# A weight load cut in two, and 26 idle matmuls moved from the tail into a wait

## The chip, the cores and the metric

The kernel runs on one core of a Trainium2 chip. The metric is the device time of one execution in microseconds. A core has TensorE (matmuls, PE in the profile), VectorE (DVE), ScalarE (ACT), GpSimd (POOL) and SyncE (SP), and 16 DMA engines that move data between the device's memory and the core.

## The reference

Two independent attention blocks, A and B, each decode one token, and their outputs are joined. Each has 32 heads of width 128 and 8192 cached keys and values per head:

```python
q = (x @ wq).reshape(B, Sq, H, Dh).transpose(0, 2, 1, 3)       # x: 1x1x512, wq: 512x4096
scores = einsum("bhqd,bhkd->bhqk", q, k_cache) * Dh ** -0.5     # k_cache: 1x32x8192x128
p = softmax(scores)
o = einsum("bhqk,bhkd->bhqd", p, v_cache)
out = o.transpose(0, 2, 1, 3).reshape(B, Sq, H * Dh) @ wo       # wo: 4096x512
```

All inputs are bf16. The caches of both blocks are 268 MB, the four weights 17 MB.

## The kernel before, in words

The 64 heads are handled in 16 rounds (`N`) of four heads (`G`), first A's eight groups and then B's. A group of K or V is 8 MB, held as 128 partitions with 64 KB each: 32 partitions (`HP`) per head, 256 keys (`T`) per partition.

Everything that is loaded in bulk goes through SP's DMA queue in the order in which SP issues it. The exception is wq of B, which ScalarE issues (its queue is q10 in the profile, SP's is q1). SP's order is: wq of A (`load_wq`, into the first half of `vn`), the two x rows, K of groups 0 and 1, and then by turns a V (`load_v`) and a K (`load_k`), each behind a wait for the buffer that it writes. K has two buffers (`kn`), V has one (`vn`). V of round n+1 is issued when the product with V of round n is done (`c_pv`), K of round n+2 when the scores of round n are done (`c_red`). At the end come wo of A, which goes into the first K buffer, the last V, and wo of B in six pieces (16, 8, 4, 2, 1 and 1 heads).

At the start TensorE turns x around (L399), waits for wq of A and multiplies (L413); ScalarE copies the queries, broadcast over partitions, into `qflat` (L368). `qflat` shares its memory with `yc`, which is used once at the end.

A round then goes like this:

- VectorE multiplies K in place with the query (L279), in two halves.
- TensorE sums that product over most of the head width with matmuls against the identity (L430, into `rps`), and VectorE sums the rest (L307).
- Maximum over the keys, across VectorE and TensorE (L312, L470, L314, L472); ScalarE takes the exponential into `pt` (L379) and its row sums.
- TensorE sums the row sums (L478), waits for V (`s_v`), and multiplies with V in 64 matmuls into `acc` (L483).
- VectorE scales and selects the result of the round before (L284 to L296), with a matmul on TensorE in between (`total_of_group`, L436).

In the last round TensorE also lays out A's and most of B's outputs and multiplies A's with wo (`mid`, L443). Behind the loop stands the tail: the first 16 heads of B with wo (L443), the function `turn_over`, `total_of_group` for the last group, and the other heads of B with wo (L505), which wait for each piece of wo in turn. VectorE and ScalarE copy the result out (L349, L384), and SP stores it (L232).

`turn_over(n)` runs n matmuls of 128x512 into `rps`, which nobody reads. Semaphores set all waits: a DMA adds 16 to its semaphore when all of it has landed.

Of the kernel before, what the change touches and what calls it, by code (L numbers as in the profile page):

```python
# [11 lines left out]
P = 128  # L12
# [33 lines left out]
def bass_concat_heads__mha_block_cached__gqa_block_cached__decode_kernel(  # L46
# [16 lines left out]
    wqs = [A_wq, B_wq]  # L63
# [4 lines left out]
    NOUT = wos[0].shape[1]  # L68
# [9 lines left out]
    N = NA * GA  # L78
# [5 lines left out]
    HM = T // 2  # L84
    W = 4
    NG = T // W


    WOB = [(0, 16, True), (16, 8, True), (24, 4, True), (28, 2, False), (30, 1, False), (31, 1, False)]
# [3 lines left out]
    with ExitStack() as st:  # L93
# [3 lines left out]
        def sb(name, shape, dt):  # L97
            return ec(nc.sbuf_tensor(name, shape, dt))

        KS = T * Dh  # L100
        kn = sb("kn", [P, 2 * KS], BF16)
        vn = sb("vn", [P, KS], BF16)
        kslot = [kn[:, i * KS:(i + 1) * KS].rearrange("p (t d) -> p t d", d=Dh) for i in range(2)]
        WQ = C * H * Dh
# [3 lines left out]
        qflat = qmem[:].bitcast(BF16)  # L108
# [10 lines left out]
        ident = sb("ident", [P, P], BF16)  # L119
# [16 lines left out]
        def ps(name, shape):  # L136
            return ec(nc.psum_tensor(name, shape, F32))

        rps = ps("rps", [P, 2, 512])
# [8 lines left out]
        def sem(name):  # L148
            return ec(nc.semaphore(name))

        s_x, s_woa, s_v, s_out = (sem(n) for n in ("s_x", "s_woa", "s_v", "s_out"))
        s_w = [sem("s_w%d" % a) for a in range(NA)]
# [25 lines left out]
            e.memset(pt[:], 0.0).then_inc(c_pool, 1)  # L178
        NPOOL = 8

        def load_wq(e, a):
            e.dma_start(vn[:, a * WQ:(a + 1) * WQ],
                        wqs[a].rearrange("(p c) n -> p (c n)", p=P)).then_inc(s_w[a], 16)


        @block.sync
        def _(e):
            load_wq(e, 0)
            for a in range(NA):
                e.dma_start(xrow[a:a + 1, :], xs[a][0]).then_inc(s_x, 16)  # L190

            def group(x, n):
                a, i = divmod(n, GA)
                return x[a][0, G * i:G * (i + 1)].rearrange("h (p t) d -> (h p) (t d)", p=HP)

            def load_k(n):
                if n >= 2:
                    e.wait_ge(c_red, RED * (n - 1))
                e.dma_start(kn[:, n % 2 * KS:(n % 2 + 1) * KS], group(ks, n)).then_inc(s_k[n % 2], 16)

            def load_v(n):
                if n:
                    e.wait_ge(c_pv, n + 1)
                else:
                    e.wait_ge(c_q, N)
                e.dma_start(vn[:], group(vs, n)).then_inc(s_v, 16)

            def load_wob(g):
                h0, n, rows = WOB[g]
                src = wos[1][h0 * Dh:(h0 + n) * Dh, :]  # L210
                dst = kn[:, WO + h0 * NOUT:WO + (h0 + n) * NOUT]
                if rows:
                    src = src.rearrange("(p j) n -> p (j n)", p=P)
                elif n > 1:
                    src = src.rearrange("(j p) n -> p j n", p=P)
                    dst = dst.rearrange("p (j n) -> p j n", j=n)
                e.dma_start(dst, src).then_inc(s_wob[g], 16)

            load_k(0)
            load_k(1)  # L220
            for n in range(N - 1):
                load_v(n)
                if n + 2 < N:
                    load_k(n + 2)
            e.wait_ge(c_red, RED * (N - 1))
            e.dma_start(kn[:, 0:WO], wos[0].rearrange("(p j) n -> p (j n)", p=P)).then_inc(s_woa, 16)
            load_v(N - 1)
            for g in range(len(WOB)):
                load_wob(g)
            e.wait_ge(c_yd, 1)  # L230
            e.wait_ge(c_ya, 2)
            e.dma_start(out[0].rearrange("o (a n) -> (o a) n", a=NA), out_sb[:]).then_inc(s_out, 16)  # L232
            e.wait_ge(s_out, 16)

        def once(e):

            one = e.alloc_register("once")
            e.reg_mov(one, 1)
            return nc.Fori(0, e.snap(one), engines=[e.engine], hint_back_edge=True)
# [111 lines left out]

        @block.scalar
        def _(e):
            load_wq(e, 1)
            with once(e):
                w_q = _Stepped(e, c_q, 1, 1)
                w_bc = _Stepped(e, c_bc, 1, 1)
                w_nb = _Stepped(e, c_nb, 1, 1)
                w_pv = _Stepped(e, c_pv, 1, 1)
                e.wait_ge(c_pv, 1)  # L360
                e.copy(xT[:].rearrange("p (a c) -> p c a", c=C),
                       misc[:, 0:C * NA].rearrange("p (c a) -> p c a", a=NA)).then_inc(c_qa, 2)
                with e.Fori(0, N // 2) as r:
                    for j in range(2):
                        w_q()
                        for h in range(G):
                            p = slice(h * HP, (h + 1) * HP)
                            i = e.copy(qflat[p, bass.ds(r * (2 * Dh) + j * Dh, Dh)],  # L368
                                       yps[j][p, h * Dh:(h + 1) * Dh])
                        i.then_inc(c_qa, 1)  # L370
                e.wait_ge(c_pool, NPOOL)
                with e.Fori(0, N):
                    w_bc()
                    e.activation(negb[:], bmp[:, 0:G], AF.Copy, scale=-scale).then_inc(c_nb, 1)  # L374
                    w_nb()
                    w_pv()
                    for h in range(G):
                        p = slice(h * HP, (h + 1) * HP)
                        e.activation(pt[p, 0:T, h], s_sb[p, :], AF.Exp, bias=negb[p, h:h + 1], scale=scale,  # L379
                                     accum_out=rsum[p, h:h + 1]).then_inc(c_p, 4)  # L380
                e.wait_ge(c_y, 1)
                e.copy(yc, yps[0][:]).then_inc(c_ya, 1)
                e.wait_ge(c_y, 2)
                e.copy(out_sb[:, NH:NOUT], yps[1][HP:HP + NA, 0:NH]).then_inc(c_ya, 1)  # L384
# [3 lines left out]
        def _(e):  # L388
            with once(e):
# [8 lines left out]
                for c in range(C):  # L398
                    i = e.matmul(misc[:, c * NA:(c + 1) * NA], xrow[:, c:D:C], ident[0:NA, 0:NA],  # L399
                                 start=True, stop=True)  # L400
                i.then_inc(c_pv, 1)
                e.wait_ge(s_w[0], 16)
                with e.Fori(0, N // 2) as r:
                    with e.If(r == GA // 2):
                        e.wait_ge(s_w[1], 16)
                    a = r // (GA // 2)
                    w0 = r * (2 * G * Dh) + a * (WQ - H * Dh)
                    x0 = a * C
                    for j in range(2):
                        e.wait_ge(c_qa, by_tile)  # L410
                        e.reg_add(by_tile, by_tile, 1)
                        for c in range(C):
# [3 lines left out]
                                start=(c == 0), stop=(c == C - 1))  # L416
# [17 lines left out]
                def total_of_group():  # L434
                    e.wait_ge(c_st, by_round)
                    e.matmul(mtp[:, EX:EX + G], om[1][:], selh[:], start=True, stop=True).then_inc(c_ex, 1)  # L436
# [21 lines left out]
                def turn_over(n):  # L458

                    with e.Fori(0, n):  # L460
                        e.matmul(rps[:, 0, :], ident[:], kn[:, 0:512], start=True, stop=True)  # L461

                with e.Fori(0, N) as r:
                    with e.Fori(0, NB // 2):
                        for tile in range(2):
                            scores(tile)
                            e.reg_add(koff, koff, HT * Dh - Dh)
                    e.reg_alu(koff, koff, 2 * KS - 1, op=ALU.bitwise_and)
                    e.wait_ge(c_g, by_round)
                    e.matmul(mtp[0:1, 0:P], m1[:], ident_f[:], start=True, stop=True).then_inc(c_gx, 1)  # L470
                    e.wait_ge(c_gm, by_round)
                    e.matmul(bmp[:, 0:G], ones_f[0:1, :], gm[:], start=True, stop=True).then_inc(c_bc, 1)  # L472
                    with e.If(r > 0):
                        total_of_group()
                    with e.If(r == N - 1):
                        mid()
                    e.wait_ge(c_p, by_round)
                    e.matmul(misc[:, 0:G], ones_f[:], rsum[:], start=True, stop=True)  # L478
                    e.wait_ge(s_v, by_round)
                    e.reg_add(by_round, by_round, 16)  # L480
                    for g in range(NG):
                        k = g % G * HP
                        m = e.matmul(acc[k:k + HP, :], ptf[:, g * W * G:g * W * G + HP],  # L483
                                     vn[:, g * W * Dh:(g + 1) * W * Dh], start=(g < G), stop=(g >= NG - G))
                    m.then_inc(c_pv, 1)
# [3 lines left out]
                for h in range(H, H + WOB[0][1]):  # L489
                    m = partial(h)  # L490
                m.then_inc(c_y, 1)
                turn_over(5)
                total_of_group()
                e.wait_ge(c_ya, 1)
                for b in range(2):
# [2 lines left out]
                for g in range(1, len(WOB)):  # L498
                    h0, n, rows = WOB[g]
                    e.wait_ge(s_wob[g], 16)  # L500
                    for h in range(h0, h0 + n):
                        for b in range(2):
                            if h == H - G - 1 and b:
# [3 lines left out]
                                         stop=(h == H - 1), skip_group_check=True)  # L507
# [29 lines left out]
```

## Time and profile before

| | |
|---|---|
| three runs | 664.8, 665.21, 665.95 us; median 665.21 |
| span of the profiled execution | 663.5 us |
| what lies around the span (median less span) | 1.7 us |
| read from the device's memory | 285.21 MB, 430 GB/s over the span |
| TensorE busy | 385.8 us (58%) |
| VectorE busy | 362.5 us (55%) |
| ScalarE busy | 76.6 us (12%) |
| critical chain, by engine | DMA 72%, PE 22%, DVE 2% |

The time of the profiled execution as such is not shown; its span, from the first to the last instruction, is. A row of a stage table gives the stage, its length, each engine's busy time with the number of instructions, the granted clock of TensorE (1.00 is full), the mean busy share of the 16 DMA engines, and what they moved. Over stages of a few microseconds that share and that rate swing, since a packet is put down to one moment; over ten and more they are steady. A row of the timeline gives start, duration, engine, line and operands, and in brackets the idle time before it and what ended that.

### The profile page before, as it was taken

What the parts mean: (1) busy time and instruction counts of PE and PEld (TensorE: products, weight loads), DVE (VectorE), ACT (ScalarE), POOL (GpSimd) and SP (SyncE); (2) the same over time, 40 slices, a digit from 0 to 9 for tenths busy, and PEclk for the clock granted to TensorE, in tenths of its full rate; (3) what the DMA queues carried; (4) which work ended last, traced back from release to release, by engine and by line L of the source; (5) the groups of instructions that cost most, each with busy time, mean ns of one, the idle gap of its engine ahead of it and who ended that gap; (6) DMA issues with size and microseconds to landing.
All of it is one profiled execution on the core that took longest, in us unless ns stands there. A gap on an engine that the chain in (4) does not pass through costs nothing.

```text
span 663.5 us, 7942 instructions
## 1 busy us (share of the span) xinstructions
PE 385.8 (58%) x2402; PEld 191.8 (29%) x2402; DVE 362.5 (55%) x249; ACT 76.6 (12%) x212; POOL 2.3 (0%) x12
## 2 busy tenths in 40 slices
PE   0455685854819185481918548191854819185488
PEld 0122232423315042330404233140423314032233
DVE  1009494848292754829274482927548292744821
ACT  0370202020010202001020200102020010202002
POOL 1000000000000000000000000000000000000000
PEclk9995988786959678695967869596786959678697
DMA  9999998999999999999999999999999999999997
GB/s 379 443 442 442 442 442 379 442 442 442 442 442 442 391 431 442 442 442 442 442 399 423 442 442 442 442 442 411 411 442 442 442 442 442 415 407 442 440 444 317
DMA packets 6041, 285.23 MB, mean 430 GB/s; under 512 B 660, under 2 KB 1176, under 8 KB 1304
## 3 DMA queue, kind: packets, MB, share of 16 engines
q1 hardware_dynamic: 5896, 281.03, 98.0%
q10 hardware_dynamic: 144, 4.19, 1.5%
q14 instruction: 1, 0.01, 0.0%
HBM read 285.21 MB, written 0.00 MB: 430 GB/s over the span
## 4 chain that ended last, share of the span: by engine, by line
DMA 72%; PE 22%; DVE 2%; issue 2%; ACT 1%; ACTq 0%; DVEq 0%; SPq 0%
DMA vn<-in_B_v_cache_dram 34%; DMA vn<-in_A_v_cache_dram 34%; PE acc L483 14%; PE rps L430 5%; DMA xrow<-in_B_x_dram 3%; PE yps L413 2%; DVE kn L279 1%; ACT qmem L368 1%; PE yps L443 1%; ACT pt L379 0%; PE yps L505 0%; DVE s_sb L307 0%; PE rps L461 0%; PE misc L478 0%; PE rps L424 0%
## 5 line engine op out<-in xcount | busy, mean ns | idle before, releaser
L279 DVE TENSOR_TENSOR kn<-kn,qmem 128x16384 bf16<-128x16384 bf16 x32 | 276.7, 8688 | 55.2 <-ACT qmem L368 43.0
L430 PE MATMUL rps<-kn,ident 128*128 x1024 | 236.8, 383 | 0.4
L483 PE MATMUL acc<-vn,pt 128*32 128x512 bf16 x1024 | 92.3, 531 | 145.7 <-DMA vn<-in_B_v_cache_dram 75.3
L307 DVE TENSOR_REDUCE s_sb<-rps 128x64 f32<-128x512 f32 x64 | 44.1, 691 | 165.1 <-PE rps L430 165.1
L430 PEld LDWEIGHTS rps<-kn,ident 128*128 128x128 bf16 x1024 | 96.4, 98 | 111.0 <-issue 22.6
L483 PEld LDWEIGHTS acc<-vn,pt 128*32 128x32 bf16 x1024 | 60.3, 127 | 171.1 <-issue 155.9
L374 ACT ACTIVATE negb<-bmp 128x4 f32<-128x4 f32 x16 | 2.8, 173 | 539.7 <-PE bmp L472 539.7
L379 ACT ACTIVATE pt<-s_sb,negb 32x256 bf16<-32x256 f32 x64 | 54.9, 858 | 4.3 <-ACT negb L374 2.9
L478 PE MATMUL misc<-rsum,ones_f 128*128 128x4 f32 x32 | 9.4, 365 | 56.4 <-ACT pt L379 56.4
L284 DVE TENSOR_SCALAR om<-acc,msk 128x128 f32<-128x128 f32 x16 | 5.6, 350 | 42.8 <-PE acc L483 42.8
L478 PEld LDWEIGHTS misc<-rsum,ones_f 128*128 128x128 f32 x32 | 8.0, 312 | 58.6 <-ACT pt L379 57.8
L413 PE MATMUL yps<-vn,xT 128*128 x64 | 17.3, 419 | 6.2 <-ACT qmem L368 4.2
L287 DVE SCALAR_TENSOR_TENSOR om<-acc,msk,om 128x128 f32<-128x128 f32 x48 | 16.8, 351 | 5.9
L470 PE MATMUL mtp<-ident_f,m 128*1 128x128 f32 x32 | 6.1, 270 | 22.6 <-DVE m L312 22.6
L424 PE MATMUL rps<-ones_bf,zrow 1*128 1x1 bf16 x64 | 11.0, 171 | 13.4 <-DVE kn L279 10.8
L424 PEld LDWEIGHTS rps<-ones_bf,zrow 1*128 1x128 bf16 x64 | 5.8, 91 | 40.6 <-issue 40.6
L368 ACT CAST qmem<-yps 32x128 f32 x64 | 16.4, 256 | 7.0 <-PE yps L413 6.3
L379 ACT ACTIVATION_READ_ACCUMULATOR pt<-s_sb,negb 32x1 f32 x64 | 15.9, 249 | 0.0
L399 PE MATMUL misc<-ident,xrow 2*128 2x2 bf16 x4 | 0.3, 166 | 22.8 <-DMA xrow<-in_B_x_dram 22.8
L413 PEld LDWEIGHTS yps<-vn,xT 128*128 x64 | 6.6, 103 | 16.5 <-issue 13.7
L472 PE MATMUL bmp<-gm,ones_f 1*128 1x4 f32 x32 | 6.1, 258 | 7.3 <-DVE gm L314 7.3
L470 PEld LDWEIGHTS mtp<-ident_f,m 128*1 128x1 f32 x32 | 1.4, 80 | 30.5 <-DVE m L312 30.5
(58 smaller groups left out, 57.0 us busy)
## 6 DMA issues: line engine op xcount, KB each, us to landing
vn<-in_B_wq_dram ACTq DMA_DIRECT2D x1, 4096.0 KB, 21.9
vn<-in_A_wq_dram SPq DMA_DIRECT2D x1, 4096.0 KB, 21.7
kn<-in_A_wo_dram SPq DMA_DIRECT2D x1, 4096.0 KB, 27.4
kn<-in_B_wo_dram SPq DMA_DIRECT2D x1, 2048.0 KB, 27.7
kn<-in_B_wo_dram SPq DMA_DIRECT2D x1, 1024.0 KB, 29.7
kn<-in_B_wo_dram SPq DMA_DIRECT2D x1, 512.0 KB, 30.5
kn<-in_B_wo_dram SPq DMA_DIRECT2D x1, 256.0 KB, 30.8
kn<-in_B_wo_dram SPq DMA_DIRECT2D x2, 128.0 KB, 30.6
```

Of the source, the lines that this page charges most:

```text
L279: e.tensor_tensor(k, k, qflat[:, bass.ds(q, Dh)].unsqueeze(1).broadcast_to([P, HM, Dh]), ALU.mult).then_inc(c_mul, 2)
L287: e.scalar_tensor_tensor(om[t % 2][:], acc[:, t * Dh:(t + 1) * Dh], msk[:, t:t + 1], om[(t + 1) % 2][:], ALU.mult, ALU.add).then_inc(*((c_ ...
L307: e.tensor_reduce(s_sb[:, h * HT:(h + 1) * HT], rps[:, h % 2, :].rearrange("p (t d) -> p t d", d=DW), AX.X, ALU.add).then_inc(c_sr, 1)
L368: i = e.copy(qflat[p, bass.ds(r * (2 * Dh) + j * Dh, Dh)], yps[j][p, h * Dh:(h + 1) * Dh])
L379: e.activation(pt[p, 0:T, h], s_sb[p, :], AF.Exp, bias=negb[p, h:h + 1], scale=scale, accum_out=rsum[p, h:h + 1]).then_inc(c_p, 4)
L413: i = e.matmul(yps[j][:], xT[:, bass.ds(x0 + c, 1)].broadcast_to([P, P]), vn[:, bass.ds(w0 + (c * H * Dh + j * G * Dh), G * Dh)], start=(c ...
L424: e.matmul(rps[:, tile, 0:1], zrow[:], ones_bf[0:1, 0:1], start=True, stop=False, skip_group_check=True)
L430: m = e.matmul(ro, ident[:], src, start=False, stop=False, skip_group_check=True)
L443: return e.matmul(yps[0][k:k + NA, :], o2[:, h, :], wo_rows(h), start=False, stop=False, skip_group_check=True)
L470: e.matmul(mtp[0:1, 0:P], m1[:], ident_f[:], start=True, stop=True).then_inc(c_gx, 1)
L478: e.matmul(misc[:, 0:G], ones_f[:], rsum[:], start=True, stop=True)
L483: m = e.matmul(acc[k:k + HP, :], ptf[:, g * W * G:g * W * G + HP], vn[:, g * W * Dh:(g + 1) * W * Dh], start=(g < G), stop=(g >= NG - G))
```

## The change

wq of A is loaded by two transfers, of partitions 0 to 15 and of 16 to 127, on the same queue and the same semaphore, so TensorE waits for 32 in place of 16. `turn_over` is called with 26 in round N - 2 ahead of the wait for V, and no longer in the tail; it reads a part of `qflat` in place of `kn`, since wo of A is being loaded into `kn` at that time.

```diff
+    NE = 16
...
-        def load_wq(e, a):
-            e.dma_start(vn[:, a * WQ:(a + 1) * WQ],
-                        wqs[a].rearrange("(p c) n -> p (c n)", p=P)).then_inc(s_w[a], 16)
+        def load_wq(e, a, p0, p1):
+            e.dma_start(vn[p0:p1, a * WQ:(a + 1) * WQ],
+                        wqs[a].rearrange("(p c) n -> p (c n)", p=P)[p0:p1]).then_inc(s_w[a], 16)
...
-            load_wq(e, 0)
+            load_wq(e, 0, 0, NE)
+            load_wq(e, 0, NE, P)
...
-            load_wq(e, 1)
+            load_wq(e, 1, 0, P)
...
-                e.wait_ge(s_w[0], 16)
+                e.wait_ge(s_w[0], 32)
...
-                        e.matmul(rps[:, 0, :], ident[:], kn[:, 0:512], start=True, stop=True)
+                        e.matmul(rps[:, 0, :], ident[:], qflat[:, 2 * NOUT:3 * NOUT], start=True, stop=True)
...
                     e.matmul(misc[:, 0:G], ones_f[:], rsum[:], start=True, stop=True)
+                    with e.If(r == N - 2):
+                        turn_over(26)
                     e.wait_ge(s_v, by_round)
...
                 m.then_inc(c_y, 1)
-                turn_over(5)
                 total_of_group()
```

## The prediction

> **What bounds the kernel now.** I read the page's DMA part first, because its share of the engines' time says whether anything else can matter.
>
> ```profile
> DMA packets 6041, 285.23 MB, mean 430 GB/s; under 512 B 660, under 2 KB 1176, under 8 KB 1304
> q1 hardware_dynamic: 5896, 281.03, 98.0%
> q10 hardware_dynamic: 144, 4.19, 1.5%
> ```
>
> The two queues together fill 99.5% of 16 DMA engines' span (98.0 + 1.5). q10 is the queue of ScalarE and holds one transfer, B's wq. It has 128 rows of 32 KB, so its 4.19 MB are 128 packets, eight for each engine, and 1.5% of 663.5 us is 9.95 us per engine: **1.24 us for a packet of 32 KB**. Next I asked for busy time by stage, to see where the 0.5% is and whether the rate ever sags.
>
> ```profile
> core 0: us, PE busy (x) PEld busy (x) DVE busy (x) ACT busy (x) POOL busy (x), PEclk, DMA share, GB/s
> 0.00:1.50 1.50, 0.00 (x0) 0.00 (x0) 0.00 (x0) 0.00 (x0) 0.84 (x8) 1.00 0.00 0
> 4.00:20.00 16.00, 0.00 (x0) 0.00 (x0) 1.50 (x13) 0.00 (x0) 0.00 (x0) 1.00 0.99 428
> 40.00:600.00 560.00, 330.70 (x2028) 167.01 (x2027) 331.79 (x199) 56.84 (x151) 0.00 (x0) 0.77 1.00 434
> 650.00:661.00 11.00, 11.00 (x139) 4.95 (x133) 1.66 (x6) 0.58 (x1) 0.00 (x0) 0.82 0.94 381
> 661.00:663.50 2.50, 0.85 (x8) 0.20 (x8) 0.41 (x1) 0.36 (x1) 0.00 (x0) 1.00 0.01 2
> ```
>
> The DMA share is 0.99 to 1.00 from the first microseconds to the last weights. Only about 1.5 us at the head and 2.5 us at the end have no traffic. So this kernel is a stream of 285 MB with a short head and a short tail; a change can win only what those two hold, and loses whatever takes the stream off its rate. The last pieces of the critical chain show what the tail waits for, and the table of waits how closely:
>
> ```profile
> 656.87 0.86 PE yps L443 x11
> 657.73 1.19 PE rps L461 x5
> 658.92 0.23 PE mtp L436 x2
> 659.15 0.53 PE yps L496 x4
> 659.68 1.90 PE yps L505 x30
> 661.61 0.29 PE yps L505 x2
> 661.92 0.41 DVE out_sb L349
> PEld yps L505 <- DMA kn<-in_B_wo_dram: 0.7, 3, 0.3
> ```
>
> TensorE waited three times, 0.7 us in all, for the last blocks of B's wo; the final pair of matmuls (661.61) starts with the last landing. TensorE is ahead of the transfers at the end, by about 0.7 us.
>
> **The change part by part.** *The head.* On SP's queue, at the start of the program, one transfer of A's wq (`vn`) becomes two; before, then after:
>
> ```order
> L182 DMA vn<-in_A_wq_dram 128x16384
> L190 DMA xrow<-in_A_x_dram 1x512
> L190 DMA xrow<-in_B_x_dram 1x512
> L199 DMA kn<-in_A_k_cache_dram 128x32768 x2
> L206 DMA vn<-in_A_v_cache_dram 128x32768
> ```
>
> ```order
> L183 DMA vn<-in_A_wq_dram 16x16384
> L183 DMA vn<-in_A_wq_dram 112x16384
> L192 DMA xrow<-in_A_x_dram 1x512
> L192 DMA xrow<-in_B_x_dram 1x512
> L201 DMA kn<-in_A_k_cache_dram 128x32768 x2
> L208 DMA vn<-in_A_v_cache_dram 128x32768
> ```
>
> Both x rows and the first two K groups move one place back, and the first transfer has 16 rows.
>
> ```profile
> 0.80 0.38 SPq L182 DMA_DIRECT2D vn<-in_A_wq_dram  x1
> 1.24 0.32 SPq L190 DMA_DIRECT2D xrow<-in_A_x_dram  x1
> 1.61 0.23 SPq L190 DMA_DIRECT2D xrow<-in_B_x_dram  x1
> 1.88 0.93 SPq L199 DMA_DIRECT2D kn<-in_A_k_cache_dram  x2
> 46.61 0.33 SPq L206 DMA_DIRECT2D vn<-in_A_v_cache_dram  x1
> vn<-in_A_wq_dram SPq DMA_DIRECT2D x1, 4096.0 KB, 21.7
> DMA to landing us min/median/max: 24.8/37.3/59.0
> ```
>
> The last row is that of the K loads (L199); its longest is the second K group, which lands at about 61 us. One more issue costs 0.23 to 0.38 us of SP. The x rows and K start that much later, but the queue already holds A's wq until 22.5 us (0.80 + 21.7), so this costs nothing. A later wq delays the queries and with them the first V's issue, but that one (46.61) comes 14 us before the queue would run empty. If the smaller first transfer is issued faster, the stream can begin earlier, by at most 0.38 - 0.23 = 0.15 us; I take -0.1.
>
> What has no row is how 16 rows move. Every large transfer here has 128 rows, eight for each engine, and all engines run side by side at 1.24 us per 32 KB. In the first piece each of the 16 engines can have one row of 32 KB (512 KB in all), and these rows are neighbours. If the way into on-chip memory belongs to an engine, the piece takes one turn, 1.24 us, as that share of the old transfer did: +0. If it belongs to a block of rows, of which each of 16 ways has eight, then 16 neighbouring rows use two ways and take eight turns: +7 x 1.24 = +8.7 us. Between these ends lie four ways and four turns: +3 x 1.24 = **+3.7 us**. Neither end has a row of its own; I take the middle halving, and keep both for the range. An engine held by a slow packet cannot take its next one from the other queue if it works packets one at a time, and the stream stands at a share of 0.99 or more afterwards, so a delay at the head is never made up: it arrives whole at the end.
>
> [...]
>
> *The round before the last.* On TensorE, between the row sums (L478, now L480) and the product with V (L483, now L487); before, then after:
>
> ```order
> L475 UNCONDITIONAL_BRANCH
> L478 MATMUL misc<-rsum,ones_f 128x4
> L480 REGISTER_ALU
> L483 MATMUL acc<-vn,pt 32x512 x64
> L463 REGISTER_ALU
> ```
>
> ```order
> L477 UNCONDITIONAL_BRANCH
> L480 MATMUL misc<-rsum,ones_f 128x4
> L481 COMPARE_AND_BRANCH
> L462 UNCONDITIONAL_BRANCH
> L463 MATMUL rps<-qmem,ident 128x512
> L462 REGISTER_ALU
> L462 COMPARE_AND_BRANCH
> L481 UNCONDITIONAL_BRANCH
> L484 REGISTER_ALU
> L487 MATMUL acc<-vn,pt 32x512 x64
> ```
>
> The loop of 26 stands ahead of the wait for V. The branch is passed in every round; it falls into that wait, or, where V has landed already (the last round), into the lead of 0.7 us.
>
> ```profile
> 608.89 17.29 DVE L279 TENSOR_TENSOR kn<-kn,qmem 128x16384 bf16<-128x16384 bf16 x2 [0.90 <-issue]
> 611.42 0.59 PE L478 MATMUL misc<-rsum,ones_f 128*128 128x4 f32 x2 [3.74 <-ACT pt L379]
> 622.54 5.73 PE L483 MATMUL acc<-vn,pt 128*32 128x512 bf16 x64 [10.53 <-DMA vn<-in_B_v_cache_dram]
> 603.00:606.20 3.20, 1.79 (x10) 0.64 (x8) 1.11 (x2) 0.00 (x0) 0.00 (x0) 1.00 0.76 328
> 606.20:609.60 3.40, 1.02 (x6) 0.62 (x6) 1.15 (x3) 1.90 (x5) 0.00 (x0) 1.00 0.93 405
> 613.00:622.50 9.50, 0.00 (x0) 0.00 (x0) 9.50 (x2) 0.00 (x0) 0.00 (x0) 0.50 0.89 386
> 622.50:626.60 4.10, 4.06 (x40) 2.87 (x44) 3.69 (x1) 0.00 (x0) 0.00 (x0) 0.50 1.09 472
> 657.70:658.80 1.10, 1.10 (x10) 0.41 (x6) 0.85 (x4) 0.58 (x1) 0.00 (x0) 1.00 0.95 387
> L461 PE MATMUL rps<-kn,ident x5: 379/379/389, 657.7 to 658.5; 128*128 128x512 bf16 x5
> ```
>
> The wait is 10.53 us. The same matmul stood in the tail five times with starts from 657.7 to 658.5, 0.2 us apart, at a granted clock of 1.00; at 0.50, which is the clock in this wait, 0.4 us. The clock rose about 4.1 us after V's matmuls began, so 26 take about 10 x 0.4 + 16 x 0.2 = 7.2 us: inside the wait. If the clock never rose, 10.4 us: still just inside.
>
> The gain: if the clock is still up when V lands, the 64 matmuls shrink: the 4.1 us at half clock become about 2.1, and 5.73 becomes 3.7 us. That brings the last V's issue and the last scores forward by up to 2.1 us, not more, because VectorE's product for the last round ends at 626.18 (608.89 + 17.29). What does it release?
>
> ```profile
> 604.76 0.33 SPq L226 DMA_DIRECT2D kn<-in_A_wo_dram  x1
> 628.30 0.33 SPq L206 DMA_DIRECT2D vn<-in_B_v_cache_dram  x1
> kn<-in_A_wo_dram SPq DMA_DIRECT2D x1, 4096.0 KB, 27.4
> ```
>
> A's wo fills the queue until 632.2 (604.76 + 27.4), so V's issue at 628.30 is already 3.9 us early; a sooner one moves no byte sooner. The last V and the wo blocks behind it land when the stream gets there. Earlier scores only add to TensorE's lead of 0.7 us. I put this edit at **0**; its cover is that queue of 3.9 us, and without it, it would be worth up to -2.1 us, or cost as much as the dummies overran V.
>
> *The tail.* On TensorE, after the last round; before, then after:
>
> ```order
> L463 COMPARE_AND_BRANCH
> L443 MATMUL yps<-kn,o 2x512 x16
> L460 UNCONDITIONAL_BRANCH
> L461 MATMUL rps<-kn,ident 128x512
> L460 REGISTER_ALU
> L460 COMPARE_AND_BRANCH
> L436 MATMUL mtp<-selh,om 128x4
> ```
>
> ```order
> L465 COMPARE_AND_BRANCH
> L445 MATMUL yps<-kn,o 2x512 x16
> L438 MATMUL mtp<-selh,om 128x4
> L499 MATMUL yps<-qmem,sel 2x256 x2
> L508 MATMUL yps<-kn,o 2x256 x32
> L391 REGISTER_ALU
> ```
>
> Five matmuls go that ran while VectorE scaled the last accumulator. L436 waits for that VectorE chain anyway, so their 1.19 us on the chain become idle: **0**. The clock could fall for want of work, but in 603.0 to 606.2 TensorE was busy 1.79 of 3.20 us and kept 1.00 through the next stretch; the drop came after 1.02 of 3.40. Without the five, the stretch around 657.7 loses about 1.1 of 3.4 us and stays at 2.3, above the row that kept it.
>
> The sum: -0.1 + 3.7 + 0 + 0 = +3.6 us. The profiled span of 663.5 would become 667.1. The runs lie 1.3 to 2.4 us above that span (664.8 to 665.95), the median 1.7; on the median 665.21 the forecast is **668.8**.
>
> **The rivals.** *The split is free (0.30).* Ways belong to engines, or an engine overlaps its two queues, so the slow piece is filled by B's wq. For it: the rate of 428 GB/s in 4 to 20 us with two queues interleaved shows no weakness. Against: nothing priced 16 rows. Then -0.1: 665.1.
>
> *The second piece suffers as well (0.24).* The 112 rows are seven per engine and need not fall as the eight do. If each of seven packets shares its way with one other, +7 x 1.24 = 8.7 more, 12.4 in all: 677.6. With a quarter of the ways for all eight packets it would be 8 x 3.7 = 30; I leave that out.
>
> *The tail's clock falls (0.04).* The 31 matmuls in 658.8 to 660.8 at half clock take 2.0 us more, of which 0.7 us of lead is covered: +1.3, 666.5. It decides only when the loss passes 0.7 us.
>
> *Faster (0.06).* In the runs that were not profiled TensorE may come late to the end: their spread is 1.15 us. If the lead from the dummies removes that much, and the head 0.15: 663.9 or a little less.
>
> **How the numbers follow.** The forecast has 0.36, with a range of its own of 667.5 to 670.5. A measurement of this kernel can tell about 0.2%, 1.3 us, from no change. Slower by more: 0.36 + 0.24 + half of the tail's clock = 0.62. Within: 0.30 + 0.02 = 0.32. Faster: 0.06. The range 664.5 to 678 holds the forecast, the free split, the tail's clock and somewhat over half of the second piece's case (0.14): 0.84.
>
> **What would show it.** Right: between 1.5 and 8 us the rate of the new profile drops well under 428 GB/s, wq of A lands 3 to 5 us later, every later V lands as much later, and the end follows. Wrong: a rate of 428 from 2 us on, with an unchanged span; or a rate that stays low up to 30 us, which is the second piece. The dummies are right if they end before V's landing and the last V is issued earlier with A's wo still in the queue; the tail, if the clock at L508 is 1.00 and TensorE still waits for wo there.

## The result, and the profile after

| | runs | median | ratio to before |
|---|---|---|---|
| before | 5 | 665.08 us (664.8 to 665.95) | |
| after | 5 | 677.42 us (677.1 to 678.03) | 1.0182 (1.017 to 1.0193) |

The change costs 12.3 us. The forecast was slower by 3.6 us (668.8); the rival in which the second piece suffers as well said 677.6. The profiled span went from 663.5 to 675.9 us, by 12.4. One run of the kernel with the matmuls alone (below) took 2037.8 us, with matmuls of L430 at 1.68 us in place of 0.38; nothing here explains it, and the ratio of that kernel leaves it out.

The first reading is where the 12 us come in. The issues of the DMA part give the time from issue to landing. Of before, the one row that the prediction does not show:

```profile
vn<-in_B_wq_dram ACTq DMA_DIRECT2D x1, 4096.0 KB, 21.9
```

Of after, the queues and the same issues:

```profile
q1 hardware_dynamic: 5912, 281.03, 97.3%
q10 hardware_dynamic: 144, 4.19, 2.1%
...
vn<-in_B_wq_dram ACTq DMA_DIRECT2D x1, 4096.0 KB, 34.2
...
vn<-in_A_wq_dram SPq DMA_DIRECT2D x1, 3584.0 KB, 34.0
...
vn<-in_A_wq_dram SPq DMA_DIRECT2D x1, 512.0 KB, 7.7
```

B's wq, which the change does not touch, landed 12.3 us later (34.2 less 21.9). That is already the whole loss, 35 us into the kernel. Its 128 packets filled 2.1% of the engines' span in place of 1.5%: 2.1% of 675.9 us is 14.2 us for eight packets on an engine, 1.77 us each, where it was 1.24. So B's packets themselves took longer; that is 4.2 us (14.2 less 9.95) for each engine. The share of both queues is 99.4%, against 99.5% before: the engines were as good as never idle, they were slow. The busy time by stage of after shows for how long (its last columns are the granted clock, the DMA share and GB/s):

```profile
1.50:4.00 2.50, 0.00 (x0) 0.00 (x0) 1.00 (x5) 0.00 (x0) 1.47 (x6) 1.00 1.43 210
4.00:8.00 4.00, 0.00 (x0) 0.00 (x0) 1.50 (x13) 0.00 (x0) 0.00 (x0) 1.00 0.86 262
8.00:20.00 12.00, 0.00 (x0) 0.00 (x0) 0.00 (x0) 0.00 (x0) 0.00 (x0) 1.00 1.00 298
20.00:40.00 20.00, 4.16 (x14) 1.53 (x15) 0.00 (x0) 2.64 (x7) 0.00 (x0) 1.00 0.99 320
8.00:33.00 25.00, 0.00 (x0) 0.00 (x0) 0.00 (x0) 0.00 (x0) 0.00 (x0) 1.00 1.05 304
60.00:600.00 540.00, 312.88 (x1930) 139.04 (x1934) 328.58 (x192) 50.58 (x126) 0.00 (x0) 0.76 1.00 433
```

As long as wq of A is on its way (it lands at about 35 us) the rate is 210 to 304 GB/s at a DMA share of about 1; the 320 of the stage from 20 to 40 us has some microseconds behind the landing in it. From 60 us on it is 433, as it was. Of before, the stretch from 8 to 33 us:

```profile
8.00:33.00 25.00, 7.68 (x27) 2.97 (x28) 0.00 (x0) 5.82 (x20) 0.00 (x0) 1.00 1.02 440
```

A rate that stays low up to 30 us is the sign that the prediction gave for the second piece. Nothing makes the head good again. The timeline of SP's issues shows the delay arrive at the end, and also the one thing that the dummies did:

```profile
638.70 0.33 SPq L208 DMA_DIRECT2D vn<-in_B_v_cache_dram  x1
674.69 0.27 SPq L234 DMA_DIRECT2D out_dram<-out_sb  x1
```

The output leaves 12.3 us later than before (674.69 against 662.37), the last V is issued only 10.4 us later (638.70 against 628.30): 2 us of lead were won there and none of it reached the end.

### The profile page after: what moved, and what is told of

The parts are those of the page before. It is cut to its first block, busy times and chain, and to the rows that moved or that the text cites. A ratio compares the mean times of both kernels' runs of the same rounds, so it can differ in the third digit from the quotient of the medians.

```text
span 675.9 us, 8043 instructions
## 1 busy us (share of the span) xinstructions
PE 391.6 (58%) x2423; PEld 170.8 (25%) x2423; DVE 362.4 (54%) x249; ACT 76.6 (11%) x212; POOL 2.3 (0%) x12
## 4 chain that ended last, share of the span: by engine, by line
DMA 77%; PE 16%; issue 3%; ACT 1%; DVE 1%; SPq 0%; ACTq 0%; DVEq 0%
DMA vn<-in_B_v_cache_dram 34%; DMA vn<-in_A_v_cache_dram 34%; PE acc L487 13%; DMA kn<-in_B_wo_dram 5%; DMA xrow<-in_B_x_dram 5%; PE yps L415 2%; PE rps L432 1%; ACT qmem L370 1%; DVE kn L281 1%; ACT pt L381 0%; PE yps L508 0%; DVE s_sb L309 0%; SPq L219 0%; SPq L183 0%; ACTq L43 0%
## 5 line engine op out<-in xcount | busy, mean ns | idle before, releaser
L487 PE MATMUL acc<-vn,pt 128*32 128x512 bf16 x1024 | 88.4, 521 | 138.3 <-DMA vn<-in_A_v_cache_dram 71.2
L487 PEld LDWEIGHTS acc<-vn,pt 128*32 128x32 bf16 x1024 | 37.6, 126 | 182.9 <-issue 175.0
L463 PE MATMUL rps<-qmem,ident 128*128 128x512 bf16 x26 | 10.1, 470 | 0.2
## 6 DMA issues: line engine op xcount, KB each, us to landing
vn<-in_B_wq_dram ACTq DMA_DIRECT2D x1, 4096.0 KB, 34.2
```

Of the source, the lines that this page charges most:

```text
L463: e.matmul(rps[:, 0, :], ident[:], qflat[:, 2 * NOUT:3 * NOUT], start=True, stop=True)
```

## The experiments

The theory, called "rows" in what was put on record: rows share ways into on-chip memory, and a piece whose rows have only a few ways moves at the rate of these few. The ways, their number and which rows share one are assumed by the author; what the runs show is the rate of a piece and the time of its packets. The rivals are named in each expectation. Each ratio is to runs of the kernel before on the same chip.

**The split alone.** The changed kernel with `turn_over(5)` back in the tail and none in the loop:

```diff
-                    with e.If(r == N - 2):
-                        turn_over(26)
...
                 m.then_inc(c_y, 1)
+                turn_over(5)
                 total_of_group()
```

> The split of wq of A alone; TensorE as before, with five matmuls in the tail. Theory 'rows' (neighbouring rows of a small piece meet on the same few ways into on-chip memory) and rival 'cut' (any second transfer costs): the whole of the loss, +12.3 us, 677.4. Rival 'TensorE' (the 26 matmuls or the bare tail cost part of it): less by what that part is; at half each, about 671.

Measured: 677.41 us, 1.0178 (1.0162 to 1.0193). The split is the whole loss. B's wq lands after 34.0 us, as in the changed kernel.

**The matmuls alone.** The kernel before with the changes of `turn_over`:

```diff
+                    with e.If(r == N - 2):
+                        turn_over(26)
                     e.wait_ge(s_v, by_round)
...
-                turn_over(5)
```

> The 26 matmuls in the last round but one and none in the tail; wq of A in one transfer. 'Rows' and 'cut': 0 within 0.5 us, since the stream behind A's wo does not wait for TensorE; the 64 matmuls with V in that round take 3.6 us in place of 5.7, and TensorE waits longer for the last weights than 0.7 us. 'TensorE': +1 us or more.

Measured: 1.000 (0.9991 to 1.0009). The matmuls cost and bring nothing. The profile is that of one more run:

> The 26 matmuls and the bare tail alone, once more for its profile. The 26 take about 10.3 us, as in the changed kernel, and end before V lands; the 64 matmuls with V take 3.6 us; the last V is issued 2 us sooner and lands when it did; TensorE waits for the last weights longer than 0.7 us; span within 0.5 us of 663.5.

Its span was 663.8 us. From its timeline and its table of waits:

```profile
611.92 10.37 PE L461 MATMUL rps<-qmem,ident 128*128 128x512 bf16 x26
622.78 3.64 PE L485 MATMUL acc<-vn,pt 128*32 128x512 bf16 x64 [0.48 <-DMA vn<-in_B_v_cache_dram]
626.45 0.33 SPq L206 DMA_DIRECT2D vn<-in_B_v_cache_dram  x1
PEld yps L506 <- DMA kn<-in_B_wo_dram: 2.2, 5, 0.7
PEld yps L443 <- DMA kn<-in_B_wo_dram: 1.7, 1, 1.7
```

The 26 fill the wait to within 0.48 us, the 64 matmuls with V take 3.64 in place of 5.73 us, and the last V is issued at 626.45 in place of 628.30. All of it ends as more waiting for wo of B: 2.2 us in five waits and 1.7 in one more, where there were 0.7 us. It is off the critical path because the stream sets the end.

**Two transfers, cut by columns.** The kernel before with wq of A in pieces of one eighth and seven eighths of the columns, all 128 rows in each:

```diff
+        def load_wq(e, a, c0, c1):
+            e.dma_start(vn[:, a * WQ + c0:a * WQ + c1],
+                        wqs[a].rearrange("(p c) n -> p (c n)", p=P)[:, c0:c1]).then_inc(s_w[a], 16)
...
+            load_wq(e, 0, 0, WQ // 8)
+            load_wq(e, 0, WQ // 8, WQ)
```

> wq of A again in two transfers of 512 KB and 3584 KB, but cut by columns: all 128 rows in both, with 4 KB and 28 KB of each row. 'Rows': 0 within 0.5 us, and the packets of a row keep the 27 GB/s of an engine. 'Cut': about +12 us, as the split by rows.

Measured: 1.0002 (0.9993 to 1.0011). The same sizes, the same number of transfers and of waits, and no loss: a second transfer as such cost nothing here. From 60 us on the rate is 433 GB/s, 27 for each of 16 engines, and from 8 to 20 us, with wq of A on its way, it is 442. "Cut" is out; what cost 12 us is the cut by rows.

**Halves.** As the split alone, with `NE = 64`.

> wq of A cut at row 64: two transfers of 64 rows, four rows for each engine in both. 'Rows', with a way for each eight rows or so: each half reaches half of the ways, its eight packets per engine take about twice 1.21 us, +6 to +12 us. Rival 'seven' (the loss comes from dealing 112 rows as seven per engine, unlike the even eight): 0 to +2 us. Rival 'cut': +12.

Measured: 678.15 us, 1.0209 (1.0182 to 1.0235), +13.0, with runs from 677.3 to 681.9; that is a little above the +6 to +12 of "rows". Two even pieces of 64 rows, four for each of 16 engines by division, cost as much as 16 and 112 (12.3). "Seven" as the only cause is out.

**Eight pieces of 16, near and far.** wq of A in eight transfers, of 16 neighbours or of every eighth row; in the third, neighbours on chip from every eighth row of the source:

```diff
+            for i in range(8):
+                load_wq(e, 0, slice(16 * i, 16 * i + 16))                     # neighbours
...
+                load_wq(e, 0, slice(i, P, 8))                                 # every eighth row
...
+                load_wq(e, 0, slice(16 * i, 16 * i + 16), slice(i, P, 8))     # to rows, from rows
```

> wq of A in eight transfers of 16 neighbouring rows each. 'Rows' at the moment of writing: each piece costs what the first piece of the changed kernel cost by its packets (its own 3.6 in place of 1.75 us and about 1 us more for B's packet behind it, 2.9), eight times 2.9 = +23 us; with full quarter rate at most 8 x 3.7 = +30. Rival 'loose dealing' (any dealing other than that of 128 rows costs alike, wherever the rows lie): +12 to +14, as with 16 and 112 and with 64 and 64.

> wq of A in eight transfers of 16 rows each, but every eighth row (0, 8, 16, ... and so on), from every eighth row of the source. 'Rows': twice as many ways as with neighbours, two turns in place of four: +7 to +13 us, clearly under the neighbours. 'Loose dealing': the same as the neighbours.

> Into 16 neighbouring rows, eight times, but each piece read from every eighth row of the source. The rows of wq land in another order than x's, so A's queries and A's half of the output differ. 'Rows' in on-chip memory: as the eight neighbours. Rival 'source' (neighbouring rows in the device's memory collide): as the eight of every eighth row, or 0.

| pieces of 16 rows | median | ratio |
|---|---|---|
| neighbours | 692.30 us | 1.0401 (1.038 to 1.0422) |
| every eighth row | 676.34 us | 1.0164 (1.0143 to 1.0186) |
| neighbours, far source | 692.92 us | 1.0412 (1.039 to 1.0434) |

Against the 665.3 of before, neighbours cost 27.0 us (3.4 for each piece) and every eighth row 11.0. Where the rows came from changed nothing (692.92 against 692.30 us); where they went did (692.30 against 676.34). "Loose dealing" and "source" are out. In the neighbours' profile there is a stretch in which B's wq has landed and the last pieces of A's run by themselves; it gives the rate of 16 neighbours:

```profile
37.40:46.60 9.20, 0.00 (x0) 0.00 (x0) 0.00 (x0) 0.00 (x0) 0.00 (x0) 1.00 1.00 114
```

114 GB/s at a DMA share of 1.00, a quarter of 433 and a little. Each of these packets of 32 KB took 4.55 us in place of 1.21, 3.8 times as long.

**Even and odd.** Two transfers of 64 rows, `slice(i, P, 2)`.

> wq of A in two transfers of 64 rows, the even ones and the odd ones. [...] If what counts is which ways a transfer reaches as a whole: 0 to +2 us. If what counts is which rows the 16 engines write at the same moment, dealt in order as four neighbours of the list for each engine: rows 0, 8, 16, ... meet in pairs on a way, as in the halves by row 64: +8 to +13 us.

Measured: 0.9998 (0.9988 to 1.0008). The stages of its profile:

```profile
4.00:8.00 4.00, 0.00 (x0) 0.00 (x0) 1.50 (x13) 0.00 (x0) 0.00 (x0) 1.00 1.01 434
```

Full rate, with B's wq beside them, for the same number of rows that cost 13 us as halves; every packet of A's wq took 1.21 or 1.22 us in the trace. The first expectation, 0 to +2 us, held in its number; no run shows what a transfer reaches, only that these two moved at the full rate. The second, which dealt the rows in order to the engines, is wrong for this shape: so dealt, the engines would have begun at rows 0, 8, ..., 120, which are the rows of one piece of the run before, and the packets of such pieces took 2.55 us where they ran by themselves.

**One queue.** The split with B's wq moved to SP, behind A's, and the same without the split:

```diff
             load_wq(e, 0, 0, NE)
             load_wq(e, 0, NE, P)
+            load_wq(e, 1, 0, P)
...
         @block.scalar
         def _(e):
-            load_wq(e, 1, 0, P)
```

> The split of 16 and 112 rows, with B's wq moved from ScalarE's queue to SP's, behind A's: each engine then has one transfer at a time, and no packet of B can meet A's on a way. To be read against the next kernel, which has one queue and no split. 'Rows': the first piece on four ways costs 4.55 in place of 1.21 us, +3.3; the 112 rows reach all ways, and if the loss in them comes from meeting B's packets they cost little more than 7 x 1.21 = 8.5 us (10.9 if dealt in order, seven neighbours to an engine): +3.3 to +6 in all. Rival 'seven' (112 rows are slow by themselves): +12 as with two queues.

> The kernel before with B's wq on SP's queue behind A's, no split: the base of the kernel with one queue. All theories: within 0.5 us of the kernel before, since the 16 engines move the same packets one after the other.

Measured: 674.50 us with the split, 1.0145 (1.0122 to 1.0169), and 665.32 without, 0.9999 (0.9989 to 1.0009). The split costs 9.2 us here: more than the 3.3 to 6 of "rows" and less than the 12 of "seven", so neither number was right. The issues of the two kernels, with the split and without:

```profile
vn<-in_A_wq_dram SPq DMA_DIRECT2D x1, 3584.0 KB, 21.1
vn<-in_A_wq_dram SPq DMA_DIRECT2D x1, 512.0 KB, 6.6
```

```profile
vn<-in_A_wq_dram SPq DMA_DIRECT2D x1, 4096.0 KB, 12.4
```

The first piece, issued at about 0.8 us, lands at 7.4; the 112 rows, issued at about 1.2, land at 22.3. That is 14.9 us for 3.67 MB, 246 GB/s, with nothing else in flight. Seven packets of 1.21 us for each of 16 engines, an estimate that deals them evenly, would be 8.5. In the trace the packets of the 112 rows took 1.68 to 3.09 us each, 2.14 in the mean, and none took 1.21: they are slow throughout, not a few of them at the end. So the 112 rows are slow by themselves, although they hold rows 32 to 95, which by themselves ran at 388 GB/s (below). The remaining 3.1 us of the 12.3 come only with B's wq on the other queue, whose packets were slower too (1.77 us in place of 1.24).

**32 and 96.** As the split alone, with `NE = 32`.

> wq of A in 32 and 96 rows, two queues. 'Rows': 32 neighbours reach eight ways, two packets for each engine at 2.2 in place of 1.21 us and B's packets behind them slower: +3 to +4; the 96 rows are six for each engine: if these behave as the 112 did (about 1.2 us for each packet of the piece), +7; together +10 to +12, 675 to 677.5. If only the first piece's few ways count: +3 to +4, 668.7.

Measured: 675.26 us, 1.0149 (1.0132 to 1.0166), +10.0, as "rows" with a price for the second piece had it; the first piece alone would have been +3 to +4. So 96 rows, six for each engine by division, are dear as well.

**64 in the middle, and every fourth row.** One queue, with A's wq in rows 32 to 95, 0 to 31 and 96 to 127; and, on two queues, four transfers of `slice(i, P, 4)`.

```diff
+            load_wq(e, 0, slice(32, 96))
+            load_wq(e, 0, slice(0, 32))
+            load_wq(e, 0, slice(96, P))
+            load_wq(e, 1, slice(0, P))
```

> One queue (B's wq behind A's on SP's): wq of A in rows 32 to 95, then 0 to 31, then 96 to 127. [...] 'Rows': the first piece runs at the full 430 GB/s, the two of 32 at half (about 2.4 us for each of two packets, twice): +4.9 us against the kernel with one queue and no split, 670.2. Rival 'neighbours' (any piece of neighbouring rows is slow): the first piece at 250 GB/s or less too, +9 or more, 674.5.

> [...] 'Rows': 0 within 0.5 us, though there are four transfers. Rival 'small pieces' (few rows cost, wherever they lie): as 32 neighbours or worse, +4 or more.

Measured: 671.37 us, 1.0125 (1.0066 to 1.0183), with a span of 669.4 against 663.9 for one queue without a split, which is +5.5 where "rows" said +4.9. Its four runs spread from 670.4 to 678.6 us, hence the wide interval; the rates below are from its profile. Every fourth row: 1.0006 (0.9997 to 1.0016). Stages of the first one's profile, about the 64 rows and about the two pieces of 32:

```profile
1.90:7.30 5.40, 0.00 (x0) 0.00 (x0) 2.50 (x16) 0.00 (x0) 1.08 (x3) 1.00 1.01 388
7.30:16.90 9.60, 0.00 (x0) 0.00 (x0) 0.00 (x0) 0.00 (x0) 0.00 (x0) 1.00 1.00 218
```

The 64 neighbours from row 32 to 95 ran at 388 GB/s with the start of the stream in it (two MB at 433 would take 4.84 of these 5.40 us); behind the first packets, all packets of the piece took 1.21 to 1.24 us in the trace. The pieces of 32 neighbours ran at 218, half of 433. "Neighbours" and "small pieces" are out: four small pieces of every fourth row cost nothing (1.0006; 434 GB/s from 4 to 8 us and 437 from 8 to 20), and 64 neighbours from row 32 ran at close to the full rate.

## Why the prediction was right or wrong

**The bound** was right. A stream at its full rate from end to end (433 GB/s at a share of 1.00 from 60 to 600 us), with nothing to win in it, turned a delay at the head into the same delay at the end: 12.3 us at 35 us, and 12.3 us at the output. The direction of the forecast was right with it, the size was not.

**The first piece** was right in size. The sum took four turns in place of one, +3.7 us, between ends of 0 and 8.7; a piece of 16 neighbours costs 3.4 us (27.0 by eight), at 114 GB/s. The choice of the middle had no row behind it; that it came out is luck as far as the rows of before go. No run shows four turns on four ways either: what the runs show is 4.55 us for a packet in place of 1.21. What the sum didn't have is that B's packets are slowed themselves, from 1.24 to 1.77 us; it only let them wait.

**The second piece** is the step that failed. The sum gave it nothing, as if 112 of 128 rows were nearly a full transfer, and put its price into a rival with 0.24. Measured, it is the larger part: 12.3 less 3.4 is 8.9 us. The error was to price the rows that the split takes out and not the 112 that it leaves behind. By themselves they move at 246 GB/s and take 14.9 us in place of 8.5; with B's wq beside them both together move at 298 to 304.

That the rival said 8.7 is in part luck. Its mechanism was that each of seven packets shares its way with one other and takes twice 1.24 us; no run shows the shared way. With one queue the second piece costs 9.2 less 3.4, or 5.8 us, and its packets took 2.14 us, not 2.48; the other 3.1 us come with B's wq on its own queue, for which the rival had no term.

What stays open is how 112 or 96 rows are dealt to the 16 engines. Rows 32 to 95, which are among them, ran at 388 GB/s by themselves, and yet every one of the 112 packets was slow (1.68 us and more with one queue); the cause was not shown. Dealing in order would explain a part for 112 rows (the expectation for one queue had 10.9 us by it, measured are 14.9), but by the same argument the even rows would have been slow, and they ran at 434. The traces name no engine for a packet.

**The 26 matmuls** cost nothing, as the sum said, and by the cover that it named: A's wo in the queue. Their length was off: 10.3 us in place of 7.2. That they came out near the 10.4 us given for a clock that never rises is luck: in the first 4 us they ran at half clock, as forecast, and then the clock did rise to 1.00, but they did not go faster than one in 0.4 us:

```profile
628.00:629.00 1.00, 0.99 (x5) 0.19 (x2) 1.00 (x1) 0.00 (x0) 0.00 (x0) 1.00 1.67 721
631.00:632.00 1.00, 0.97 (x4) 0.25 (x3) 1.00 (x1) 0.00 (x0) 0.00 (x0) 1.00 0.76 328
632.00:633.00 1.00, 0.96 (x3) 0.23 (x3) 1.00 (x1) 0.00 (x0) 0.00 (x0) 1.00 0.15 66
L463 PE MATMUL rps<-qmem,ident x26: 379/390/634, 624.1 to 634.0; 128*128 128x512 bf16 x26
PEld rps L463 <- issue: 7.4, 24, 0.4
```

These are stages of the changed kernel. Two or three matmuls start in each microsecond (a count takes in one that began before), where the five of the old tail started 0.2 us apart. A matmul's own duration is the same in both, 0.38 to 0.39 us in the median; the five overlapped, the 26 did not. Ahead of 24 of the 26 weight loads (PEld) there is idle time, 0.31 us in the mean, for which the profile shows no cause ("issue"). Why the 26 did not start as close together as the five was not shown.

**The tail** cost nothing: with the dummies alone the ratio was 1.000, and TensorE waited 2.2 us in place of 0.7 for the last weights. In the changed kernel the chain ends like this:

```profile
640.02 32.63 DMA kn<-in_B_wo_dram
672.65 0.04 issue
672.69 0.60 PE yps L508 x8
673.29 0.00 issue
673.29 0.61 PE yps L508 x6
673.91 0.02 issue
673.93 0.29 PE yps L508 x2
674.22 0.02 issue
674.24 0.41 DVE out_sb L351
```

Where the tail of before ran back through L443 and L461 on TensorE, this one runs straight into the weights' transfer. The granted clock over these last matmuls, from 672.6 to 674.3 us, was 1.00. The rivals "tail's clock", "free" and "faster" are out.

## What to carry to other kernels

Before a transfer is cut, ask which rows each piece still holds, and ask it of the piece that stays as well as of the one that goes: a cut by columns, by even and odd rows or by every fourth row was free here, cuts into blocks of rows cost 6 to 27 us on 4 MB. In a kernel whose DMA share is 1.00 throughout, as here, busy share does not show a lost rate: look at GB/s by stage (304 at a share of 1.05 from 8 to 33 us, where it was 440 at 1.02) and at the time to landing of a transfer that the change did not touch. Where transfers set the end, as here, ask what an earlier engine will wait for next: TensorE's 2 us of lead came to nothing, and its waits for the last weights went from 0.7 to 2.2 us and 1.7 more.

## What the runs showed of the hardware that was not expected

- More rows were not faster: 64 even rows ran at 434 GB/s (with B's wq beside them), pieces of every fourth row lost nothing (1.0006), and 112 rows ran at 246 GB/s, with 2.14 us for a packet in place of 1.21.
- Beside a slow transfer another queue's packets were slower: B's went from 1.24 to 1.77 us beside the 16 and 112 rows, and to 1.33 beside even and odd rows (1.6% of 664.0 us).
- 64 rows from 0 and 64 rows from 32 differ: halves cut at row 64 cost 13 us, while rows 32 to 95 ran at 388 GB/s, close to the full rate, and the two pieces of 32 rows behind them at 218.
- The loss went with the rows that are written, not with those that are read: the same pieces read from every eighth row of the source gave 692.9 against 692.3 us, and written to every eighth row as well 676.3.
- The loop of 26 matmuls of 128x512 issued one in 0.4 us at a granted clock of 1.00, where the five of the old tail started 0.2 us apart, also at 1.00.
